# A fused attention and gated feed-forward kernel: a third of the feature transposes by DMA, with changed head order, array-division priorities, tail pieces and copies

## The chip, the cores and the metric

One Trainium2 chip, one core of it. The metric is the device time of one execution in microseconds (us), and the kernel's output is compared with the reference in every run. A ratio in this document is the mean time of one kernel's fast runs over the mean of the other's fast runs of the same rounds on the same chip, with a 95% interval, so it isn't quite the ratio of the medians that are quoted. "Fast" is the undisturbed state of the chip.

The engines: TensorE (PE: matmuls; PEld: its weight loads), VectorE (DVE), ScalarE (ACT), GpSimd (POOL), SyncE (SP, which here only issues DMAs; its queue is SPq). "The span" is the time from the first to the last instruction in the trace; it is 1.7 us shorter than the time of the same execution.

## The reference, cut to what matters

```python
# q, k, v: (4 batches, 8 heads, 768 positions, 64);  heads 0, 2, 6 are "retrieval" heads
scores = (q @ k.T) / 8
mask   = causal                              # retrieval heads
         causal & (sink(4) | window(64))     # the other five heads
x      = softmax(scores, mask) @ v           # -> (3072 tokens, 512)
g      = x @ w_gate;  val = x @ w_val        # 512 -> 1536
ffn    = (gelu(g) * val) @ w_out             # 1536 -> 512
out    = x + sigmoid(x @ w_res) * ffn        # float32
```

The attention result `x` has tokens in the partitions (rows). The projections contract over the 512 features, so they need `x` with features in the partitions: every 128x128 block of `x` must be transposed.

## The kernel before

The kernel writes down some 1,700 tasks and lets a list scheduler, run when the program is built, put them in a fixed order on each engine. 3,072 tokens go through in six chunks of four tiles of 128. The heads go in pairs. After two pairs (four heads) half of a chunk's features are there, and they are transposed by TensorE:

```python
PAIRS = ((0, 2), (4, 6), (1, 3), (5, 7))
ORDER = (0, 2, 1, 3)                   # heads 0 to 3 first, then 4 to 7
...
def to_features(c, cb, pr, x16, xdeps, xtbuf, xttoks, l0, n):
    scr = Buf(P_ps, "scr")
    tp = G.add("pe", c_mm(128, n), lambda e: [e.transpose(          # n = 4 blocks of 128x128
        out=at16(scr)[:, i * 128:(i + 1) * 128], in_=at(x16)[:, cb % 2, i, :], identity=ident[:, :]) for i in range(n)],
        xdeps + [t_ident], pr - 3, bufs=[x16, scr], name="xT")
    ...
    te = G.flex({"dve": (..., ev("dve")), "act": (..., ev("act"))}, # PSUM -> SBUF, by VectorE or ScalarE
                [tp], pr - 3, bufs=[scr, xtbuf], name="xE")
```

The projections then read one half of the features after the other, 512 tokens wide (`w` is the gate or the value weight; from the second chunk on, the first halves may run before the second half is there):

```python
for c0 in (0, 2):
    xd = [t for cb, t in xttoks if c0 <= cb < c0 + 2]
    tg = G.add("pe", c_mm(512, 2), mk(wg, gb, c0), xd + [wtok["g", f // 4], tg], pr, ...)
    tv = G.add("pe", c_mm(512, 2), mk(wv, vb, c0), xd + [wtok["v", f // 4], tv], pr, ...)
```

A matmul uses either the full 128x128 array or a part of it (scores: 64 rows; window products: 64 columns). The scheduler's first criterion on TensorE is to stay in the division that it is in; the second is a priority per task, of which 127 are overridden by a hand-tuned list of pairs "task number : priority":

```python
key = (int(e == "pe" and mode is not None and t.mode != mode), t.prio, t.seq)
...
for x in "".join(HINTS).split():
    n_, p_ = x.split(":")
    G.tasks[int(n_)].prio = float(p_)
```

The last tile's output product is done in two pieces of 256 columns, so that VectorE can finish the first while TensorE does the second:

```python
for w in ((slice(0, 256), slice(256, 512)) if last else (slice(0, 512),)):
    ...  # 12 matmuls into PSUM, then two VectorE passes (times the gate, plus x), then a store
```

In the start, VectorE makes small helpers from the first values: four "sink" copies (`vk`, 4 rows of 130 elements) and copies shifted by 64 rows (`vs`).

The softmax here doesn't subtract the row's maximum and nothing guards it: scores larger than these inputs give would overflow.

## Time and profile before

| kernel before | value |
|---|---|
| time, median of three runs | 274.97 us (274.32 to 275.02) |
| span of the profiled execution | 273.0 us (its time 274.70) |
| TensorE busy | 98% |
| first projection starts | 20.50 us |
| last matmul starts | 269.58 us |
| start of the last matmul to the end of the span | 3.40 us |

The prediction below shows the lines for TensorE's share and its chain. Two groups matter beside them. The columns are line, engine, operation, names, shapes, count; then busy time in us and the mean of one record in ns; then idle time just before them.

```profile
L994 PE MATMUL ps<-ident,x 128*128 128x128 f16 x96 | 8.1, 219 | 0.0
L1083 PE MATMUL ps<-wo,hT 128*128 128x256 f16 x24 | 3.0, 273 | 0.0
```

L994 is the transposes: 96 of them, with a record of 219 ns each. A record runs from a matmul's start to its modelled end, and the next one starts long before that end. What a transpose occupies is the distance from its start to the next start, 0.056 us. L1083 at 256 columns is the last tile's output in its two pieces.

### The profile page before, as it was taken

The numbers are of one execution on the slowest core, as the hardware profiler recorded it, in microseconds if no ns is written. First come the engines' busy times: TensorE is split into PE (matmuls) and PEld (weight loads), VectorE is DVE, ScalarE is ACT, GpSimd is POOL, SyncE is SP. The second block draws the span as 40 slices with busy tenths as digits, with TensorE's granted clock in tenths as the row PEclk, the third lists the DMA queues.
The fourth block names the chain that finished last, engine by engine and source line by source line (L and its number), as shares of the span: only waits on it lengthen the run. The fifth ranks groups of instructions, "written<-read, shape, count | busy, mean of one in ns | idle before, by whom it ended". The sixth has DMA issues, their size and how long they took to land.

```text
span 273.0 us, 5729 instructions
## 1 busy us (share of the span) xinstructions
PE 266.8 (98%) x2413; PEld 140.7 (52%) x2413; DVE 141.5 (52%) x275; ACT 144.0 (53%) x222; POOL 85.8 (31%) x120
## 2 busy tenths in 40 slices
PE   6999999999999999999999999999999999999995
PEld 5777654465444355444455444456444355544443
DVE  2798353387345358353278335366443447625344
ACT  2795356775434775435674432877234877424310
POOL 8999239995461078970000000000000000000000
DMA  6999999999999999999611000121010010110022
GB/s 87 170 206 207 183 185 226 163 159 179 177 187 151 151 161 194 192 186 136 136 42 72 7 0 0 41 80 40 2 38 0 2 62 17 42 38 0 0 79 77
DMA packets 92474, 27.81 MB, mean 102 GB/s; under 512 B 81184, under 2 KB 88864, under 8 KB 92448
## 3 DMA queue, kind: packets, MB, share of 16 engines
q0 software_dynamic: 70320, 14.69, 63.0%
q1 hardware_dynamic: 22128, 12.76, 23.8%
q8 instruction: 19, 0.31, 0.5%
q14 instruction: 7, 0.06, 0.1%
HBM read 29.36 MB, written 6.29 MB: 131 GB/s over the span
## 4 chain that ended last, share of the span: by engine, by line
PE 89%; DMA 5%; POOL 4%; issue 1%; DVE 0%; POOLq 0%
PE ps L1040 43%; PE ps L1083 23%; PE ps L1068 8%; DMA wg<-in_moe_w_gate_dram 5%; PE ps L794 5%; PE ps L927 3%; PE ps L917 2%; PE ps L994 2%; PE ps L941 1%; PE ps L1022 1%; POOL qks L540 1%; POOL va L540 1%; PE ps L653 1%; PE ps L885 1%; POOL wg L540 1%
## 5 line engine op out<-in xcount | busy, mean ns | idle before, releaser
L1054 DVE SCALAR_TENSOR_TENSOR hT<-gact,ps 128x512 f16<-128x512 f16 x68 | 45.6, 686 | 65.2 <-ACT gact L1052 33.8
L1052 ACT ACTIVATE gact<-ps 128x512 f16<-128x512 f32 x68 | 40.4, 597 | 66.7 <-PE ps L1040 57.5
L1040 PE MATMUL ps<-xT,wg 128*128 128x512 f16 x272 | 73.3, 379 | 0.3 <-DMA wg<-in_moe_w_gate_dram 0.3
L1040 PE MATMUL ps<-xT,wv 128*128 128x512 f16 x272 | 73.3, 379 | 0.0
L1083 PE MATMUL ps<-wo,hT 128*128 128x512 f16 (+1 forms) x300 | 70.8, 371 | 0.0
L1040 PEld LDWEIGHTS ps<-xT,wg 128*128 128x128 f16 x272 | 26.2, 98 | 31.2 <-DMA wg<-in_moe_w_gate_dram 0.6
L1040 PEld LDWEIGHTS ps<-xT,wv 128*128 128x128 f16 x272 | 26.3, 98 | 30.7 <-ACT gact L1052 0.4
L1083 PEld LDWEIGHTS ps<-wo,hT 128*128 128x128 f16 x300 | 27.1, 98 | 27.7 <-issue 1.3
L540 POOL DMA_DIRECT2D qks<-in_k_dram x36 | 28.7, 838 | 30.7 <-DMA qkt<-qks 20.9
L810 ACT ACTIVATE er<-ps 128x1024 f16<-128x1024 f32 (+4 forms) x40 | 34.4, 891 | 7.3 <-PE ps L794 6.9
L1087 DVE SCALAR_TENSOR_TENSOR otile<-srs,ps 128x512 f32<-128x512 f32 (+1 forms) x25 | 16.6, 664 | 25.0 <-PE ps L1083 24.8
L540 POOL DMA_DIRECT2D qks<-in_q_dram x36 | 29.0, 851 | 0.8 <-POOLq L1179 0.8
L1068 PE MATMUL ps<-wr,xT 128*128 128x512 f16 x96 | 24.7, 379 | 0.0
L1071 ACT ACTIVATE srs<-ps 128x512 f32<-128x512 f32 x24 | 14.3, 596 | 17.0 <-PE ps L1068 16.9
L540 POOL DMA_DIRECT2D va<-in_v_dram x24 | 21.4, 936 | 3.4 <-PE ps L941 3.4
L794 PE MATMUL ps<-qkt 64*128 64x64 f16 (+4 forms) x399 | 17.9, 215 | 0.0
L980 DVE TENSOR_TENSOR xtok<-ps,rcp 128x512 f32<-128x512 f32 (+1 forms) x28 | 16.9, 608 | 0.5
L1090 DVE TENSOR_TENSOR otile<-otile,xtok 128x512 f32<-128x512 f32 (+1 forms) x25 | 16.7, 669 | 0.7
L1001 ACT ACTIVATE xT<-ps 128x512 f16<-128x512 f16 (+1 forms) x19 | 9.8, 538 | 12.6 <-PE ps L994 12.6
L794 PEld LDWEIGHTS ps<-qkt 64*128 64x128 f16 x399 | 10.4, 94 | 8.9 <-issue 4.2
L1100 PE MATMUL ps<-blank 128*128 128x128 f16 x118 | 11.2, 241 | 2.6 <-DVE blank L514 2.6
L1068 PEld LDWEIGHTS ps<-wr,xT 128*128 128x128 f16 x96 | 8.7, 98 | 9.8 <-issue 0.7
(67 smaller groups left out, 221.6 us busy)
## 6 DMA issues: line engine op xcount, KB each, us to landing
out_dram<-otile SPq DMA_DIRECT2D x23, 256.0 KB, 2.4
va<-in_v_dram POOLq DMA_DIRECT2D x24, 128.0 KB, 18.7
qks<-in_k_dram POOLq DMA_DIRECT2D x32, 64.0 KB, 13.7
qks<-in_q_dram POOLq DMA_DIRECT2D x32, 64.0 KB, 13.7
wg<-in_moe_w_gate_dram POOLq DMA_DIRECT2D x3, 512.0 KB, 10.4
wv<-in_moe_w_val_dram POOLq DMA_DIRECT2D x3, 512.0 KB, 12.3
wo<-in_moe_w_out_dram POOLq DMA_DIRECT2D x4, 384.0 KB, 23.9
vs<-va SPq DMA_DIRECT2D x4, 260.0 KB, 5.4
```

The source lines that it names most:

```text
L540: return G.add(eng, issue, lambda e: e.dma_start(out_ap(), in_ap), deps, prio, bufs=bufs, dma=cost, name=name, grp=grp)
L794: return [e.matmul(at(scr)[:, oo:oo + w], lhsT=at(BB.qkt)[half, 1, p, k0:k0 + 128], rhs=at(BB.qkt)[half, 0, p, qq:qq + w], start=True, sto ...
L810: return e.activation(out=o, in_=i_, func=AF.Exp, scale=SM_SCALE)
L980: t2 = G.add("dve", c_dve(2 * n * 64), lambda e: e.tensor_tensor(out=xview(), in0=avv(0, DHEAD), in1=scale(), op=ALU.mult), [t1] + xdeps, ...
L1040: return lambda e: [e.matmul(at(dst)[:, :], lhsT=w[:, ci, f * 128:(f + 1) * 128], rhs=at(xtbuf)[:, ci, :], start=(ci == 0), stop=(ci == NC ...
L1052: ta = G.add("act", c_act(512), (lambda gb=gb, ga=ga: lambda e: e.activation(out=at(ga)[:, :], in_=at(gb)[:, :], func=AF.Gelu))(), [tg], p ...
L1054: th = G.add("dve", c_dve(512), (lambda vb=vb, ga=ga, f=f: lambda e: e.scalar_tensor_tensor(out=at(h)[:, f, :], in0=at(ga)[:, :], scalar=0 ...
L1068: e.matmul(at(rb)[:, :], lhsT=at(xtbuf)[:, ci, s], rhs=wr[:, ci, :], start=(ci == 0), stop=(ci == NCB - 1))
L1071: ta = G.add("act", c_act(512), (lambda rb=rb, sr=sr: lambda e: e.activation(out=at(sr)[:, :], in_=at(rb)[:, :], func=AF.Tanh, scale=0.5)) ...
L1083: e.matmul(at(fb)[:, w], lhsT=at(h)[:, fi, s], rhs=wo[:, fi, w], start=(fi == 0), stop=(fi == NF - 1))
L1087: t1 = G.add("dve", c_dve(n), (lambda fb=fb, sr=sr, ot=ot, w=w: lambda e: e.scalar_tensor_tensor(out=at(ot)[:, w], in0=at(sr)[:, w], scala ...
L1090: t2 = G.add("dve", c_dve(n), (lambda ot=ot, lt=lt, w=w: lambda e: e.tensor_tensor(out=at(ot)[:, w], in0=at(ot)[:, w], in1=at(xbuf)[:, lt, ...
```

## The change

The intent: TensorE is full, so take work from it. Half of the transposes from the third chunk on are done by the DMA engines, from SBUF to SBUF and without PSUM. As a DMA takes longer than a transpose on TensorE, the heads whose half goes by DMA (4 to 7) come first, and heads 0 to 3, still transposed on TensorE, come second. The remaining parts are small: a second priority ("swap") for tasks that would change the array's division, three pieces for the last tile, and lighter work for VectorE in the start.

```diff
+LATER = (1, 3, 0, 2)                     # heads 4 to 7 first, then 0 to 3
+DT_FIRST = 2
 HINTS = ( ... )                          # a new list, tuned for the new graph
+SWAP = -3000.0
+VS_DMA = 1
...
-key = (int(e == "pe" and mode is not None and t.mode != mode), t.prio, t.seq)
+away = e == "pe" and mode is not None and t.mode != mode
+p_ = t.prio if t.swap is None or not away else t.swap
+key = (int(away), p_, t.seq)
...
-t.alts = {"dve": t.alts["dve"]}          # first batch's sink copies on VectorE
+t.eng, t.alts, t.prio = "pool", None, VK_AT
...
-for lo, hi, pr in ((1, 2, -75), (2, 4, 130)):   # value shifts of the start on VectorE
+for lo, hi, pr in ((1, 2, -75),) + (() if VS_DMA else ((2, 4, 130),)):   # the second pair by DMA
...
+order = ORDER if c < DT_FIRST else LATER
...
-for cb in (P.heads[0] // 2, P.heads[1] // 2):
+if c >= DT_FIRST and P.p == order[1]:
+    to_features_dma(c, P.heads[0] // 2, P.pr, x16, xdeps, xtbuf, xttoks)
+else:
+  for cb in (P.heads[0] // 2, P.heads[1] // 2):
       to_features(c, cb, P.pr, x16, xdeps, xtbuf, xttoks, l0, len(tiles))
...
+def to_features_dma(c, cb, pr, x16, xdeps, xtbuf, xttoks):
+    t = G.add("sp", 1.3, lambda e: e.dma_start(          # 8 blocks of 128x128, fp16
+        at(xtbuf)[:, cb:cb + 2, :]..., at(x16)[:, :, :, :]..., transpose=True), xdeps, pr - 4003, ...)
...
+TAIL = (slice(0, 256), slice(256, 384), slice(384, 512))
-for w in ((slice(0, 256), slice(256, 512)) if last else (slice(0, 512),)):
+for w in (TAIL if last else (slice(0, 512),)):
...
+for t in G.tasks:
+    if t.mode is not None:
+        t.swap = t.prio + SWAP
```

Cut: the masks of the start are made in two parts, and the two heads of a pair no longer wait for each other where they write different halves of PSUM.

## The prediction

> **What bounds the kernel now.** I read the page's engine shares and slices first, then the chain of waits in order of time, then the timeline of TensorE (start to start), the waits by engine and the DMA view.
>
> ```profile
> PE 266.8 (98%) x2413; PEld 140.7 (52%) x2413; DVE 141.5 (52%) x275; ACT 144.0 (53%) x222; POOL 85.8 (31%) x120
> PE   6999999999999999999999999999999999999995
> PE 89%; DMA 5%; POOL 4%; issue 1%; DVE 0%; POOLq 0%
> ```
>
> TensorE is busy in every slice but the first and last; the others are near half. Busy alone proves little, so here is the chain (start, length, what):
>
> ```profile
> 13.20 14.06 DMA wg<-in_moe_w_gate_dram
> 27.30 1.04 PE ps L1040 x4
> ...
> 90.64 1.40 PE ps L1083 x6
> 92.04 0.54 PE ps L794 x6
> 92.58 0.97 PE ps L1068 x4
> 93.55 1.29 PE ps L1083 x6
> ...
> 109.67 0.45 PE ps L994 x8
> 110.11 20.29 PE ps L1040 x94
> ...
> 264.86 5.00 PE ps L1083 x34
> 269.89 0.43 DVE otile L1087
> 270.34 0.42 DVE otile L1090
> ```
>
> From 27.30 to 269.86 us the chain is TensorE alone. L1040 runs at 20.29/94 = 0.216 us a matmul, though its record says 379 ns: records overlap, and the spacing is the cost. Almost nothing there waits; the waits by engine put only 0.3 us on a matmul for a weight (gate, third load, landing at 27.3). So the time is three parts: a start to the first projection at 20.50 us, 249.4 us of packed TensorE, and a tail of 3.1 us (two DVE passes and the store).
>
> The start is packed too: TensorE has few visible gaps from 2.64 to 20.50 us, since 118 filler matmuls on zeros (L1100) lie between the real ones. Their number is fixed when the program is built: **making the other engines faster in the start brings the first projection forward only if the new program also has fewer fillers.**
>
> **What the Trainium skill says.** *TensorEngine Tiling (Array Packing)*, Tiling Modes, Key Properties: changing the tiling mode drains TensorE. The trace agrees and gives the size: six L1083 matmuls take 1.29 us after full-array work but 1.40 us after a divided stretch, four L1068 take 0.86 or 0.97. So each return to the full array costs 0.11 us. *TensorE: Matmul & The Clock Gate*, Part 4, gives a TensorE transpose as about 275 ns in a kernel. Here the record says 219 ns, but eight take 0.45 us in the chain, 0.056 us each; the spacing decides what removing one is worth. *DMA: Bandwidth & Descriptors*, Issuing engines are not separate DMA queues: all DMAs interleave on the same 16 engines. The trace agrees: the same 4-block DMA transpose lands in 2.5 to 2.9 us at 128 to 131 us, when loads have ended, but in 5.6 to 9.5 us while they run. *GPSIMD Engine Reference*, Performance versus the Vector engine: GpSimd is slower for elementwise work. No GpSimd copy is in this trace; its other small operations of 64 to 128 columns take 0.20 to 0.30 us.
>
> **The change part by part.** I compared the instruction orders of the two kernels, engine by engine.
>
> *Transposes by DMA.* In chunks three to six, half of the features (heads 4 to 7) leave TensorE: 96 transposes become 64, and eight PSUM evictions go (28 to 20). 32 x 0.056 = **-1.8 us** on the packed engine. The evictions (about 0.54 us each on ACT) save nothing, as ACT is at 53%. Four 8-block DMA transposes on the SP queue replace them, each hidden if it lands in time (below). Doing heads 4 to 7 first only buys that time.
>
> *Swap priorities.* Counting returns to the full array in the two orders: 18 before the first projection and 40 after it, total 58; in the changed kernel 15 and 39, total 54. 4 x 0.11 = **-0.4 us**. All changes of division together fall only from 126 to 122: a small effect.
>
> *Last tile in three.* The last piece is 128 columns instead of 256. One DVE pass costs 0.69 us at 512 and 0.43 at 256 columns, so by the same slope 0.29 at 128. Two passes: -0.27 us. The store shrinks from 128 to 64 KB; 256 KB land in a median 2.4 us and 128 KB in 1.7, so perhaps another 0.1. TensorE does 24 matmuls of 128 columns (0.056 us, as the transposes) in place of 12 of 256 (0.109): +0.03. Together **-0.3 us**.
>
> *Sink copies to GpSimd, value shifts to DMA, masks in parts.* These take four sink copies (1.2 us, some stretched) and two shift copies (0.5 and 0.4 us) from DVE, which is nearly full between 10 and 20 us. But the program has 119 fillers instead of 118, and 43 instead of 34 stand before the first query arrives: after 34 the trace already waits only 0.2 us for that load, so the first real matmul will be some 0.4 us later, made up by eight fewer later. The first projection now comes with eight fewer window and two fewer sink products done; those 0.3 us reappear later. Start: **about 0**, +0.06 for the filler. On GpSimd the four copies (estimate 1.0 us, from its 0.2 to 0.3 us operations) delay three weight loads' issue; these stand in a queue anyway (second gate load issued at 11.7, landing at 22.2), so this is hidden.
>
> *The weight wait.* The old order uses the third gate weight 6.5 us after the first projection. By my sum the new order has about 10 us of work ahead of it, so the 0.3 us wait goes: **-0.3 us**. The two shift DMAs (130 KB each) share the engines with the weights, about 1.3 us at the 200 GB/s of these slices, so the first value weight, landing at 19.6, may come at 20.5 and cost some tenths.
>
> Sum: -1.8 - 0.4 - 0.3 + 0.06 - 0.3 = -2.7 us, if nothing new waits.
>
> **The rivals.**
>
> *A. The DMA transpose lands late and TensorE waits for it.* From the end of heads 5 and 7's products to the first matmul that reads their half, the new order has 10.4 to 11.1 us of TensorE work (tasks at measured spacings). Reciprocal, scaling and semaphores take about 1.2 us, so some 9.3 us are left for issue and landing. A 4-block transpose takes 1.2 to 1.8 us on the SP queue in most cases; twice the blocks are an estimated 2.5 us or more. In chunks four to six loads have ended: an estimated 4 to 5 us, no wait. In chunk three (about 100 to 110 us) other transposes and loads share the engines and 4 blocks take 7.4 us: the landing may be 0 to 3 us late. I charge **+0.5 us**. If the small size of the data units slows even the quiet ones past 9.3 us, all four wait, perhaps 3 us each, and the time is 280 or more. The 2.5 us landings speak against that.
>
> *B. The start becomes the gain.* If freeing DVE brings the first half's features forward and PE was waiting unseen among the fillers, the first projection could come 1 us sooner, 271.2 us. For it: DVE nearly full in 10 to 20 us. Against: fillers unchanged in number, and the value weight lands at 19.6 at the earliest.
>
> *C. The start becomes a loss.* The shift DMAs delay the weights, and GpSimd waits for the first value tile in front of three weight issues. That makes 0.5 to 1.5 us, 273 to 274 us. For it: DMA near full until 125 us. Against: weights are used later in the new order.
>
> *D. Nothing is won.* TensorE might have been limited by ACT or DVE through the projections, so removed transposes turn into waits. Against: 94 matmuls at 0.216 us without a gap.
>
> **How the range and chances follow.** 274.97 - 2.7 + 0.5 = 272.7 us; rounded to 272.6. The low end: no late transpose and half a microsecond from B, 271.2. The high end: A and C together add 2 us, 274.6. Faster by over 2% needs under 269.5, 5.5 us off, twice what the counts hold: 2%. Slower by over 2% needs 280.5, all four transposes late: 3%. The rest is within 2%.
>
> **What would show each step right or wrong.** Right: 64 transposes at L994's successor and 28 - 8 evictions; packed TensorE from the first projection shorter by about 2.3 us; the chain still TensorE alone, without a DMA entry for the xT tile; xT DMA landings under 9 us; projection matmuls still 0.216 us; last DVE passes near 0.29 us; first projection at 20 to 20.8 us. Wrong: a wait of TensorE on the xT DMA (A), a first projection before 19.5 (B) or after 21 (C), or projections in waits on ACT or DVE (D). The prediction falls if the four DMA transposes interact with stores or loads so that each lands more than 10 us after issue, or if one in-order queue holds something urgent behind them.

## The result, and the profile after

The changed kernel takes 273.11 us (273.08 to 273.62, four runs) against 274.99 (274.32 to 275.02, four runs) for the kernel before in the same rounds: a ratio of 0.9942 [0.9923, 0.9961]. That is 0.6% faster, within the band of 2%, and 0.5 us above the predicted 272.6. The spans of the profiled executions are 271.4 and 273.0 us. They differ by 1.6 us and the medians by 1.9, as the profiled execution of the kernel before (274.70 us) was a fast one of its kind.

The page of the changed kernel, its engine shares, TensorE's slices and the sum of the chain:

```profile
PE 265.2 (98%) x2394; PEld 138.8 (51%) x2394; DVE 140.5 (52%) x272; ACT 139.9 (52%) x214; POOL 87.0 (32%) x124
PE   7989999999999999999999999999999999999995
PE 88%; DMA 6%; DVE 1%; POOL 0%; issue 0%; DVEq 0%
```

TensorE is as full as before with 19 matmuls fewer (32 transposes gone, 12 more for the tail in 128s, one more filler). ACT lost 4 us of evictions, from 144.0 to 139.9, and the time shows nothing of that: it was no bound. DMA has a larger part in the chain, and the chain in order of time (start, length, what) shows why:

```profile
11.02 9.33 DMA wv<-in_moe_w_val_dram
...
20.40 1.92 PE ps L1054 x16
...
103.04 0.31 PE ps L947 x11
103.36 7.67 DMA xT<-x
...
111.08 19.60 PE ps L1072 x90
```

The chain before went through the third gate weight's load, landing at 27.3 us; this one goes through the first value weight's, landing at 20.35. At 103.36 us it leaves TensorE for a DMA: the transpose of chunk three's first half. TensorE was working beside that DMA for most of its 7.67 us, but the DMA ended last. The waits by engine (us in total, times, longest) put a size to both:

```profile
PE ps L1054 <- DMA wv<-in_moe_w_val_dram: 1.1, 1, 1.1
PE ps L1072 <- DMA xT<-x: 0.6, 1, 0.6
```

The groups that answer to the two shown of the kernel before:

```profile
L1026 PE MATMUL ps<-ident,x 128*128 128x128 f16 x64 | 5.5, 219 | 0.0
L1117 PE MATMUL ps<-wo,hT 128*128 128x128 f16 x24 | 1.5, 219 | 0.0
```

Every one of the matmuls is in both traces, so the time can be counted from their starts. For each matmul, take the distance to the next start. In undisturbed runs of one kind it is 0.216 us at 512 columns, 0.109 at 256, 0.056 at 128 and for the transposes. What exceeds the usual spacing (the median of its kind) at a change of division is its cost; what exceeds it by over 0.05 us between two matmuls on the full array is a stall.

| counted from the matmul starts, us | before | changed | difference |
|---|---|---|---|
| first projection starts | 20.50 | 20.40 | -0.10 |
| from there to the start of the last matmul | 249.07 | 247.93 | -1.14 |
| of it, transposes (88 and 56) | 4.91 | 3.12 | -1.79 |
| of it, changes of division (88 and 88) | 9.58 | 9.58 | 0.00 |
| of it, stalls | 0.59 | 0.95 | +0.35 |
| of it, window and sink products that used to be before the first projection (estimate: they fill 20.18 to 20.50 us before) | | | +0.3 |
| start of the last matmul to the end of the span | 3.40 | 3.06 | -0.34 |
| span | 273.0 | 271.4 | -1.6 |

The four inner rows give -1.1, all of the -1.14. (A change of division costs 0.109 us on average here. With the smallest spacing of each kind as the usual one it would be 11.1 and 11.2 us, or 0.126 each, the figure in the expectations below; the difference between the kernels stays at 0.1 or less.) The stalls before are 0.47 us for the third gate weight (the page's 0.3; the page counts from the modelled end of a record, the spacing from the starts) and one of 0.13. In the changed kernel they are 0.76 us for the DMA transpose (the page's 0.6) and one of 0.18 near the end.

The start needs its own reading. The changed kernel's last filler starts at 19.05 us and TensorE is ready at about 19.2; the first value weight lands at 20.35, where before it landed at 19.63. So TensorE was ready more than a microsecond sooner, and the later weight took it back. Some 0.3 us of that are the products moved past the first projection. The rest fits a VectorE that is sooner done: its last scaling pass ahead of the first half's last transposes starts at 16.52 us instead of 18.74, and those transposes at 18.28 instead of 19.39. But the new order of the start changed with it, and no run separates the two. On GpSimd the four sink copies took 0.28 to 0.40 us each; on VectorE they had taken 0.19 to 0.45.

### The profile page after: what moved, and what is told of

The parts are those of the page before. It is cut to its first block, busy times and chain, and to the rows that moved or that the text cites. A ratio compares the mean times of both kernels' runs of the same rounds, so it can differ in the third digit from the quotient of the medians.

```text
span 271.4 us, 5681 instructions
## 1 busy us (share of the span) xinstructions
PE 265.2 (98%) x2394; PEld 138.8 (51%) x2394; DVE 140.5 (52%) x272; ACT 139.9 (52%) x214; POOL 87.0 (32%) x124
## 4 chain that ended last, share of the span: by engine, by line
PE 88%; DMA 6%; DVE 1%; POOL 0%; issue 0%; DVEq 0%
PE ps L1072 43%; PE ps L1117 22%; PE ps L1102 7%; PE ps L813 5%; DMA wv<-in_moe_w_val_dram 3%; DMA xT<-x 3%; PE ps L1054 3%; PE ps L947 3%; PE ps L937 2%; PE ps L961 1%; PE ps L1026 1%; PE ps L668 1%; PE ps L904 1%; DVE otile L1124 0%; DVE otile L1121 0%; POOL wg L549 0%
## 5 line engine op out<-in xcount | busy, mean ns | idle before, releaser
L1072 PE MATMUL ps<-xT,wg 128*128 128x512 f16 x272 | 74.7, 379 | 0.6 <-DMA xT<-x 0.6
L1072 PE MATMUL ps<-xT,wv 128*128 128x512 f16 x272 | 74.2, 379 | 0.0
L1117 PE MATMUL ps<-wo,hT 128*128 128x512 f16 (+2 forms) x312 | 70.0, 363 | 0.0
L1121 DVE SCALAR_TENSOR_TENSOR otile<-srs,ps 128x512 f32<-128x512 f32 (+2 forms) x26 | 16.7, 643 | 14.6 <-PE ps L1117 12.2
L813 PE MATMUL ps<-qkt 64*128 64x64 f16 (+3 forms) x399 | 17.9, 215 | 0.0
L1124 DVE TENSOR_TENSOR otile<-otile,xtok 128x512 f32<-128x512 f32 (+2 forms) x26 | 16.8, 648 | 0.8
L829 ACT ACTIVATE es<-ps 128x1024 f16<-128x1024 f32 (+1 forms) x14 | 12.6, 898 | 1.3 <-PE ps L813 1.1
```

What stands on the lines that cost most here:

```text
L813: return [e.matmul(at(scr)[:, oo:oo + w], lhsT=at(BB.qkt)[half, 1, p, k0:k0 + 128], rhs=at(BB.qkt)[half, 0, p, qq:qq + w], start=True, sto ...
L829: return e.activation(out=o, in_=i_, func=AF.Exp, scale=SM_SCALE)
L1072: return lambda e: [e.matmul(at(dst)[:, :], lhsT=w[:, ci, f * 128:(f + 1) * 128], rhs=at(xtbuf)[:, ci, :], start=(ci == 0), stop=(ci == NC ...
L1117: e.matmul(at(fb)[:, w], lhsT=at(h)[:, fi, s], rhs=wo[:, fi, w], start=(fi == 0), stop=(fi == NF - 1))
L1121: t1 = G.add("dve", c_dve(n), (lambda fb=fb, sr=sr, ot=ot, w=w: lambda e: e.scalar_tensor_tensor(out=at(ot)[:, w], in0=at(sr)[:, w], scala ...
L1124: t2 = G.add("dve", c_dve(n), (lambda ot=ot, lt=lt, w=w: lambda e: e.tensor_tensor(out=at(ot)[:, w], in0=at(ot)[:, w], in1=at(xbuf)[:, lt, ...
```

## The experiments

All gave correct outputs. Each is compared with runs of the kernel before on the same chip (medians 274.97 to 274.99 us). All are edits of the changed kernel except one, which is an edit of the kernel before.

### 1. All transposes back on TensorE, head order kept (te_all)

```diff
-if c >= DT_FIRST and P.p == order[1]:
+if False and P.p == order[1]:      # the added tasks are left out of the hints' numbering
```

> The changed kernel with heads 4 to 7 still first, but transposed by TensorE in all chunks. Theory (what a removed transpose saves is its spacing on the packed TensorE, 0.056 us, and the one late DMA transpose gives part of it back): 32 transposes more cost 1.8 us, the 0.76 us stall in the third chunk goes, four more changes of array division cost 0.5 us: about 1.5 us over the changed kernel, 274.6 us. Rival (the evictions taken off ScalarE and VectorE were worth something too, or the record's 219 ns is what counts): 32 x 0.219 = 7 us or at least over 3 us slower.

Measured: 279.79 us (278.56 to 280.10), ratio 1.0174 [1.0149, 1.0199]. That is 6.7 us over the changed kernel, near the rival's 7, but neither account explains it. From first projection to last matmul it takes 253.31 us, 5.4 more than the changed kernel: 1.79 for the 32 transposes (0.056 each, as counted), 0.32 for four more changes of division, and the rest nearly all new stalls of TensorE, 4.1 us against 0.9. The timeline of TensorE in the last chunk (start, length, what; in brackets what it waited for) shows the largest:

```profile
235.71 0.41 PE L965 MATMUL ps<-vk,ek 128*128 128x65 f16 x8
237.92 0.61 PE L1030 MATMUL ps<-ident,x 128*128 128x128 f16 x8 [1.79 <-DVE x L1006]
239.13 0.59 PE L1076 MATMUL ps<-xT,wg 128*128 128x512 f16 x2 [0.61 <-DVE xT L1037]
```

The transposes wait 1.79 us for VectorE to scale the heads, then the projection waits for the eviction. What follows: the order in the program was tuned for a graph in which this half needs no transposes on TensorE and no evictions. Putting them back leaves the order wrong as well, so this run prices the DMA transposes *together with* the order, not alone. Run 9 was made to price a transpose without touching the order.

### 2. Only chunk three's transposes back on TensorE (te_c2)

```diff
-if c >= DT_FIRST and P.p == order[1]:
+if c > DT_FIRST and P.p == order[1]:
```

> The changed kernel with the third chunk alone transposed by TensorE, the three later chunks by DMA. Theory: the third chunk's DMA transpose lost 0.76 us of TensorE time and saved 8 x 0.056 = 0.45 us, so without it -0.3 us; the new schedule has three more changes of division, +0.4 us; together within 0.3 us of the changed kernel, and no TensorE wait on a DMA in the third chunk. Rival (the wait only hides another one behind it): a stall of about the same size appears at the same place for another reason, and the time is 0.5 us or more over the changed kernel.

Measured: 274.41 us (274.26 to 274.62), ratio 0.9987 [0.9972, 1.0002], so slower than the changed kernel by half a per cent. The 0.76 us stall on the DMA is gone, but a new one has come in the next chunk: 1.02 us at 150 us. Its chain (start, length, what):

```profile
150.04 0.69 DVE otile L1125
150.73 0.35 DVE xT L1037
```

An eviction of features on VectorE stands behind a 0.69 us pass over an output tile, and TensorE waits for the eviction. The rival holds here in kind and size, though the new stall is in the next chunk and not at the same place: even chunk three's DMA transpose, late as it is, is better than what stands in its place in this order.

### 3. No swap priorities (no_swap)

```diff
-t.swap = t.prio + SWAP
+t.swap = None
```

> The changed kernel without the separate priorities between array divisions, all else equal. In its instruction order there are 97 changes of division after the first projection instead of 88. Theory (each change costs about 0.126 us of TensorE, as in both traces, and the rule matters only through their number): +1.1 us, 274.2 us. Rival (changes hide behind other waits, or the rule delays something): no difference over 0.3 us.

Measured: 276.69 us (276.63 to 276.93), ratio 1.0071 [1.0056, 1.0086]. After the first projection there are 97 changes of division instead of 88, costing 10.41 us instead of 9.58. That +0.83 us is the direct effect. The other loss is stalls, 3.4 us instead of 0.9, in eight places of the rescheduled order. So the rule is needed *in this graph with these hints*. It isn't a gain over the kernel before, which reaches the same 88 changes without the rule, by its own hints.

### 4. Last tile in two pieces (tail2)

```diff
-TAIL = (slice(0, 256), slice(256, 384), slice(384, 512))
+TAIL = (slice(0, 256), slice(256, 512))
```

> The changed kernel with the last tile in two pieces of 256 columns, as before; the rest of the order is the same. Theory: the last two VectorE passes take 0.43 us instead of 0.29 us each and the store is 128 KB instead of 64 KB: the end is 0.3 us later, 273.4 us. Rival (VectorE was already behind at the end, three pieces mean six short passes): no difference, or two pieces are faster.

Measured: 273.01 us (272.77 to 274.91), ratio 0.9956 [0.9916, 0.9996]; the changed kernel's own ratio was 0.9942. The times alone can't tell the two apart. The trace can: from the start of the last matmul to the end of the span it is 3.39 us with two pieces and 3.06 with three. The 0.3 us is hidden in the time of the profiled execution because the first value weight landed 0.4 us sooner there, so that the first projection started at 19.96 instead of 20.40 us. The last VectorE passes of the changed kernel, for comparison with those at L1087 and L1090 that the prediction shows (start, length, what):

```profile
268.67 0.28 DVE L1121 SCALAR_TENSOR_TENSOR otile<-srs,ps 128x128 f32<-128x128 f32 x1
268.98 0.29 DVE L1124 TENSOR_TENSOR otile<-otile,xtok 128x128 f32<-128x128 f32 x1
```

The predicted 0.29 us a pass was right.

### 5. Gate before value in the first four projections (g_first)

If TensorE waits at 19.2 us only because the value weight is late, then doing the two gate projections first, whose weight has landed, should win the wait back.

```diff
-first four projections in the order v0 g0 v1 g1
+first four projections in the order g0 g1 v0 v1     # all else in its place
```

> The changed kernel with only the first four projections reordered from value, gate, value, gate to gate, gate, value, value; every other instruction keeps its place. Theory (TensorE was ready at 19.28 us and waited 1.12 us for the first value weight, although the first gate weight had landed at about 17 us): two gate groups of 0.44 us each fill the wait, 0.2 us of it is left, the whole is 0.9 us faster, 272.2 us. Rival (the first part is bound by something else too, such as the activation of the first gate or the features of the second half): the gain is given back within a few us and the time stays within 0.3 us.

Measured: 273.46 us (272.57 to 274.07), ratio 0.9939 [0.9901, 0.9976]: no change. The first projection starts at 19.20 us, 1.2 earlier, but the last matmul starts only 0.3 us earlier than in the changed kernel. The waits (us in total, times, longest):

```profile
PE ps L1072 <- DMA wv<-in_moe_w_val_dram: 0.4, 1, 0.4
PE ps L1054 <- DMA wv<-in_moe_w_val_dram: 0.3, 1, 0.3
```

The wait has moved to the next value weights: 0.45 us at 19.96 and 0.52 at 25.05, counted by starts. The rival's forecast, no gain, held, though the activation and the features that it names were not the bound: it is the arrival of the weights as a whole that binds the start, not the one place where TensorE meets it.

### 6. The two shift DMAs held back until the first value weight has landed (vs_late)

This tests rival C, that the DMA shifts delay the weights. The order of instructions is kept; the two shifts also wait for the weight.

```diff
+for t in held: t.deps.append(wtok["v", 0])     # held: the two shift DMAs of the start
```

> The changed kernel, same order, but the two value-shift DMAs of the start wait until the first value weight has landed. It measures the contention. Theory (the shift DMAs took engine time from the weights): the first value weight lands near 19.6 us as in the kernel before, instead of 20.35, and the first projection starts then; later TensorE waits some 2 us for the shifts, so the whole is slower by 1 to 2 us. Rival (the later landing comes from the GpSimd copies or from run to run): it lands at 20.3 us all the same.

Measured in one look (state unknown): 278.82 us. On the disputed point it is clear: the first value weight lands at 19.52 us instead of 20.35, and the first projection starts at 19.57. Then the shifts, which TensorE needs next, are late. The chain (start, length, what):

```profile
11.03 8.50 DMA wv<-in_moe_w_val_dram
...
20.21 5.59 DMA vs<-va
25.84 0.43 PE ps L939 x8
```

TensorE waits 4.62 us for them (counted by starts; the profile has 4.35 of idle time), and the granted clock, the share of the full TensorE clock that the chip allows, is half for 6.83 us from 25.66 on: 256-column matmuls are spaced 0.21 us instead of 0.109. The theory on contention held (0.8 us); the total was spoilt by the experiment's own new wait.

### 7. The kernel before with the DMA transpose alone (before_xd)

```diff
+if c >= 2 and P.p == ORDER[1]:
+    to_features_dma(...)               # heads 0 to 3, which come first in the kernel before
+else: ...                              # hints keep their task numbers
```

> The kernel before with the DMA transpose alone: heads in the old order, so that heads 0 to 3 are done first and are the ones transposed by DMA in chunks three to six. Theory (heads 4 to 7 first only buys time for the landing): the first matmul that needs the half comes only 6.2 us of TensorE work after its last product in the third chunk and 4.5 to 5.8 us in the others; issue and landing took 7.7 us there and 3.1 to 3.4 us later, with 1.2 us of VectorE before: a stall of 2 to 3 us in the third chunk, none to 0.3 us in the later ones. 275.0 - 1.8 + 2.5 + 0.4 for three more changes of division = 276.1 us. Rival (the order of heads is irrelevant to the DMA transpose): no stall, 273.6 us.

Measured: 290.61 us (290.38 to 291.48), ratio 1.0563 [1.0536, 1.0590]. Slower by far more than expected. Windows of the profiled execution around chunk three's transpose (window, its length, then busy time and count of PE, PEld, DVE, ACT, POOL, then granted clock, DMA share, GB/s; the share adds up the time of packets that overlap and can exceed 1):

```profile
109.60:114.20 4.60, 0.28 (x5) 0.10 (x2) 1.74 (x4) 0.60 (x1) 4.60 (x7) 0.74 1.89 168
114.20:118.50 4.30, 4.28 (x11) 1.52 (x12) 0.00 (x0) 0.60 (x1) 4.30 (x6) 0.50 1.68 190
118.50:124.00 5.50, 5.50 (x27) 2.53 (x26) 1.87 (x3) 1.71 (x3) 2.19 (x3) 0.99 1.83 182
```

TensorE idles for 4.6 us, 4.35 of them on the DMA. Then it is busy, but its granted clock is 0.50: 11 matmuls in 4.3 us, and in the third window 27 in 5.5. Ten of 512 columns at 0.43 us instead of 0.216 cost another 2.1 us. The Trainium skill has this: *TensorE: Matmul & The Clock Gate*, Part 1, has a full and a half clock in its table of states, and the half after an idle window of about 3.4 us. The traces agree: 4.35 us of idle time, here and in run 6, came with 6.83 us of half clock each. They add something: a second stretch at half clock here, from 203.93 to 207.34 us, follows two shorter waits in a row, 2.08 and 1.12 us in the timeline, so one single long wait isn't needed. The waits on VectorE's scaling (2.28, 1.65, 1.31, 1.31, 1.06, 0.77 and 0.71 us from one start to the next) and that stretch make up much of the rest. So the DMA transposes alone aren't a gain but a loss of 16 us here. Only chunk three's wait is one for the DMA itself; the three later transposes landed in 3.0 us and nothing waited for them. The waits on VectorE belong to the order that the scheduler made of the altered graph.

### 8. The changed kernel with the old head order (low_first)

```diff
-LATER = (1, 3, 0, 2)
+LATER = (0, 2, 1, 3)
```

> The changed kernel with the old order of heads in every chunk, so that the DMA transposes heads 0 to 3. In its instruction order the half is needed 1.9 us of TensorE work after its last product in the third chunk and 6.6 to 7.7 us in the later ones. Theory: a stall of about 7 us in the third chunk, none later, and eight more changes of division (1.0 us): about 280 us. Rival: the order of heads brings nothing by itself, under 275 us.

Measured in one look (state unknown): 289.62 us. The wait on the DMA transpose is over 5.6 us at 116 us, and there are 96 changes of division. TensorE also waits 6.8 us in all on VectorE's scaling, and the half clock, from 111.62 to 125.27 us, begins with these waits (1.81 and 1.82 us at 106 and 109 us), before the long one. So the sentence in the prediction that the head order "only buys that time" has the right mechanism, but the time bought is worth more than the transposes themselves: the wait on the DMA alone, 5.9 us by starts, is three times their 1.8. As the hints were tuned for the other order, part of these 16 us may be due to them; this run can't say how much.

### 9. Twice as many transposes on TensorE, nothing else (xt_twice)

Every remaining transpose from chunk three on is done twice, first into the unused half of the same PSUM buffer. The order is unchanged, so this measures the price of 32 transposes alone.

```diff
-... for i in range(n)]
+... for o in ((4, 0) if c >= DT_FIRST else (0,)) for i in range(n)]     # out column (o + i) * 128
```

> The changed kernel, same instruction order, in which each TensorE transpose that is left in chunks three to six is done twice (the first copy goes to an unused half of its PSUM bank): 32 transposes more, no eviction more. It measures the term that the prediction gave to the removed transposes. Theory (spacing counts, 0.056 us each): 1.8 us over the changed kernel. Rival 1 (the record's 219 ns counts): +7 us. Rival 2 (TensorE has hidden slack there): under +0.8 us.

Measured: 274.10 us (273.82 to 274.52), ratio 0.9969 [0.9953, 0.9985], about 1.0 us above the changed kernel. By starts, the 32 added transposes take 1.78 us, 0.0556 each, and not the 219 ns of the record, which would be 7 us. The net is +1.02 us between first projection and last matmul, because the stall of 0.76 us on the DMA transpose has gone: the added work in front of it hides it. In the waits of this run only the value weight is left:

```profile
PE ps L1055 <- DMA wv<-in_moe_w_val_dram: 0.7, 1, 0.7
```

This is the cleanest measure of the change's main term, and also shows how a removed cost uncovers a wait.

### 10. Chunk three's DMA transpose three places earlier in SP's queue (xd_early)

In the prediction the transpose was late because others "share the engines". SP's own timeline in the changed kernel (start, length, what) shows something beside that:

```profile
95.44 6.06 SPq L706 DMA_TRANSPOSE qkt<-qks  x4
101.54 0.59 SPq L1128 DMA_DIRECT2D out_dram<-otile  x1
102.18 1.13 SPq L628 DMA_DIRECT2D vs<-va  x2
103.36 1.77 SPq L1017 DMA_TRANSPOSE xT<-x  x1
```

Its data were ready at 100.92 us (the last product of heads 5 and 7 ended at 99.5; a reciprocal, a mask and the scaling on VectorE follow), but the queue is in order and issued the last of four query/key transposes, a store and two shifts first. The edit moves it ahead of those three.

```diff
 SP's order:  4 query/key transposes
+             xT transpose of chunk three
              store of an output tile, two value shifts
-             xT transpose of chunk three
```

> The changed kernel, same order but for the SP queue, where the first DMA transpose of features (third chunk) is issued ahead of the three ordinary DMAs (one store, two value shifts) that stood before it. Theory (the transpose was ready at about 100.6 us but issued only at 103.36 us, because the SP queue is in order): it is issued 1.5 to 2 us sooner, lands sooner, the 0.76 us stall of TensorE goes: -0.7 us against the changed kernel, if the start is the same. Rival (the landing is slow because the engines are shared): the stall stays over 0.5 us.

Measured: 272.40 us (271.84 to 272.90), ratio 0.9901 [0.9884, 0.9919]. SP's timeline in this run:

```profile
101.53 1.23 SPq L1017 DMA_TRANSPOSE xT<-x  x1
102.81 0.80 SPq L1128 DMA_DIRECT2D out_dram<-otile  x1
103.66 1.12 SPq L628 DMA_DIRECT2D vs<-va  x2
```

It issues 1.8 us sooner, at 101.53, as soon as the scaling is done (101.51). The stall is gone, and from the first projection to the last matmul it takes 247.16 us, 0.77 less than the changed kernel, the size of the stall. The span of this profiled execution, 271.2 us, hides that: its first projection came 0.6 us later than in the changed kernel, on a value weight that landed late again.

It did not land faster as far as the trace shows. The DMA view of the changed kernel gives a landing for it (the last number), and that of this run none:

```profile
xT<-x SPq DMA_TRANSPOSE x1, 7.7
xT<-x SPq DMA_TRANSPOSE x1
```

Only 14 of its 16 semaphore updates are in the trace, the last at 108.08 us, so it took at least 6.5 us; the first matmul that reads the half starts at 110.90 without a wait. In run 12, which has it at the same place in the queue, it took 6.5 us. In the ten kernels where the record is complete, chunk three's transpose lands in 6.4 to 9.7 us, and those of the later chunks in 3.0 to 3.8. What differs is the traffic (the changed kernel from issue to landing, chunks three and four; columns as in run 7):

```profile
103.36:111.03 7.67, 7.12 (x82) 3.80 (x78) 5.66 (x11) 2.82 (x5) 7.67 (x11) 1.00 1.70 174
142.58:145.65 3.07, 3.07 (x33) 1.70 (x32) 2.49 (x5) 1.65 (x3) 0.00 (x0) 1.00 0.44 85
```

So the stall took two things: a landing of over 6 us in the stretch where loads still run, and an issue 2.4 us after the data were ready. Run 10 shows that taking away the second is enough. The rival was wrong about the stall but not about the landing, which stayed slow; that the shared engines make it slow fits the traffic, and no run tested it.

### 11. The two value shifts of the start on VectorE instead of DMA (shift_dve)

```diff
-two shift DMAs of the start on SP
+two copies on VectorE, just before the first window product that needs them
```

> The changed kernel, same order, with the two value shifts of the start as VectorE copies in place of DMAs, put where VectorE idles (about 20.4 us). Theory (the shift DMAs delay the weights, seen in the run that held them back): the first value weight lands at 19.6 us instead of 20.0 to 20.7 and all later weights likewise; first projection 0.4 to 1.1 us sooner, -0.6 us in all. Rival (the later weights bind in any case): the first projection comes sooner but a wait for a later weight takes it back.

Measured: 272.43 us (271.72 to 272.89), ratio 0.9901 [0.9882, 0.9920]. The first value weight lands 8.3 us after its issue instead of 9.3, and the first projection starts at 19.38, 1.0 us sooner than in the changed kernel. The rest of the program takes as long (247.97): it holds a new wait of 0.64 us for the VectorE copies, and the stall on chunk three's transpose shrinks to 0.36. Over all kernels the first value weight takes 8.9 to 9.9 us where the shift DMAs are in the start (nine kernels) and 8.3 to 8.6 where they aren't or come later (five). The two groups don't overlap, and their means lie 0.9 us apart. That settles the mechanism of rival C.

### 12. Runs 5, 10 and 11 together (best)

> The changed kernel with three moves in its fixed order: gate, gate, value, value at the start; the first DMA transpose of features ahead of three DMAs; the two value shifts on VectorE. Theory: -0.9 to -1.3 us at the start, as the weights no longer wait for the shifts and TensorE has gate work until they land, and -0.7 us in the third chunk: 271.2 us, 1.4% under the kernel before. Rival (weight arrival is the bound of the whole start): only the third chunk's 0.7 us and a few tenths, 272.2 us.

Measured: 271.83 us (271.72 to 272.75, five runs), ratio 0.9888 [0.9872, 0.9904]. It beats both kernels: by 1.1% the one before, by about 0.5% the changed one. Against run 10 or run 11 alone the intervals overlap, so the three moves together aren't shown to beat either, and the time lies between theory (271.2) and rival (272.2). What still stands in its way can be seen in its start, VectorE and then TensorE:

```profile
20.55 1.20 DVE L637 COPY vs<-va 64x1040 f16<-64x1040 f16 x2
...
21.80 0.22 PE L942 MATMUL ps<-vs,es 128*64 128x65 f16 x1 [0.62 <-DVE vs L637]
```

The shift copies start at 20.55 us, just before the product that needs them, and TensorE waits 0.62 us. Placing them earlier on VectorE was not tried.

## Why the prediction was right, and where it was not

The range and the direction were right; the time was 0.5 us too low, 0.1 of it a slip of the sum (274.97 - 2.7 + 0.5 is 272.7 or 272.8, not 272.6). Of its signs, these came true: 64 transposes, landings under 9 us, projections at 0.216 us, last passes near 0.29 us, the first projection at 20.40. Two did not: the packed part became shorter by 1.14 us and not by 2.3, and the chain has a DMA entry for xT. By its own terms:

| term | predicted, us | shown, us | by |
|---|---|---|---|
| 32 transposes | -1.8 | -1.79 | starts, run 9 |
| swap priorities | -0.4 | 0.0 | starts, run 3 |
| last tile in three | -0.3 | -0.3 | starts, run 4 |
| start, with the products moved past it | about 0, +0.06 | -0.10 + 0.3 | starts, runs 5, 6, 11 |
| weight wait | -0.3 | -0.47 at its old place | starts |
| late DMA transpose | +0.5 | +0.76 | starts, run 10 |

**The transposes** were priced right, because the spacing was used and not the record. Run 9 shows it without any change of order.

**The swap priorities** are the term that failed. The prediction counted 58 returns to the full array in the old order and 54 in the new, and charged 0.11 us for each of the four. By its own count three of these were before the first projection (18 to 15), where TensorE fills its time with zeros and, in the changed kernel, waits 1.1 us for a weight in any case. After it one return went (40 to 39), but all changes of division together stayed at 88, and so did their cost, 9.58 us. The step was wrong in its own terms: a saving must be counted where the engine is the bound, and over all changes. Had this been done, the sum would have been 273.1, the measured time; that would have been partly luck, as three other terms were off by 0.1 to 0.3 us with different signs.

**The tail** came out as worked.

**The start** came out near zero for a reason that the prediction had put under two rivals, B and C, and not in its sum: both happened and nearly cancelled, which is luck. B: TensorE was ready at about 19.2 us, over a microsecond sooner. C: the first value weight landed 0.7 us later, and runs 6 and 11 show that the shift DMAs delay it. One side step was plainly wrong: the first real matmul was to come 0.4 us later, because more fillers stand before it, but it came at 5.68 us instead of 5.96. The fillers begin at 1.06 us instead of 2.64, as VectorE clears their zeros sooner. The 0.3 us of the products moved past the first projection fits what the rows leave, and was not measured by itself.

**The weight wait** went from the third gate weight, as predicted, but waiting as such didn't go: the first value weight took its place, in the start.

**Rival A** was right in place (chunk three), kind (a wait of TensorE on the DMA) and roughly in size. Its cause was put down to shared engines alone, and the prediction allowed no time for standing in SP's queue. There the transpose stood 2.4 us behind others, and run 10, which takes this away, has no stall. (The prediction did name an in-order queue as a danger, but for what stands behind the transposes.) The slow landing itself was as it said, 7.7 us against 7.4. One of its readings was loose: of the 4-block transposes that land while loads run, one took 5.2 us, not 5.6 or more; and eight blocks took 1.2 to 2.3 us on the queue in the changed kernel, not 2.5 or more. The three later DMA transposes cost no wait, and the median landing of the four is 3.4 us, better than the "estimated 4 to 5".

**Rival D** was wrong: the projections are still spaced at 0.216 us, and the evictions saved on ACT bought nothing.

What stays open: how much of the losses in runs 1, 3, 7 and 8 comes from hints that fit another graph, which only tuning them again could tell; how much of the earlier start is due to VectorE; what makes chunk three's transpose land slowly; and why the first value weight's landing varies by up to a microsecond among kernels whose starts are the same.

## What to carry to other kernels

Price work taken from a busy TensorE by the distance between starts, and only in the stretch where TensorE is the bound; savings in a stretch that waits for a load are worth nothing. An in-order DMA queue is a schedule of its own: look at what stands ahead of an urgent DMA as well as at the traffic beside it, and keep small convenience DMAs out of the phase in which weights arrive. Priorities tuned by hand belong to one graph: undoing one part of a tuned change measures the part and the mistuning together, so an experiment that adds work without moving anything is worth more.

## What the Trainium skill lacked or had wrong

- *TensorE: Matmul & The Clock Gate*, Part 2, Back-to-back issue gap, gives a sustained spacing of about 81 ns at 128 columns and 131 ns at 512 for streams of weight load and matmul. This kernel is such a stream (as many weight loads as matmuls), and its spacing is 56 and 216 ns, which is what the same page calls the isolated gap.
- The same page, Part 4, says that full clock doesn't engage for transposes. Here the transposes stand 56 ns apart between matmuls at full clock, like any matmul of 128 columns (1.78 us for 32, run 9). Whether transposes alone would bring the clock to full, no run shows.
- *TensorEngine Tiling (Array Packing)*, Tiling Modes, Key Properties, says that a change of mode drains the array, but not what it costs: 0.109 us on average here (9.58 us for 88).
- *DMA: Bandwidth & Descriptors*, DMA Transpose (X-bar), has no duration for an issue or a landing from SBUF to SBUF at this size: eight 128x128 blocks of fp16 occupied SP's queue for 1.2 us when it was quiet and landed 3.0 to 3.8 us after issue in chunks four to six, but 6.4 to 9.7 us in chunk three, where loads still ran.
- The same page, Queues, rings and completion order, treats the order of completion, and I found no warning that the issuing engine's own order can hold an urgent DMA back: here for 2.4 us from its data being ready to its issue, of which 1.8 behind a store and two shifts.
